# Hash-bucketed attention and two MLPs on one core: attention's result kept in feature rows, 32-column hash tiles, one rounding operation for k and q

## The chip, the cores and the metric

The kernel runs on one core of a Trainium2 chip. The metric is device time in microseconds (us). The kernel before takes 785.51 us (median of three runs, 785.46 to 785.63). The profiled execution took 787.35 us, and its span, from the first to the last instruction, is 785.6 us.

## The reference

Attention over 2 batches of 8 heads, 768 tokens, head size 64. A query sees only the keys of its own bucket; the bucket is given by the signs of six random projections. The result goes through two MLPs (1536 tokens, 512 to 2048 to 512), the first with softplus, the second with x * relu6(x + 3) / 6. The weights are float64.

```python
q_bits = (np.einsum('bhsd,dk->bhsk', q, proj) > 0)       # proj: 64 x 6
k_bits = (np.einsum('bhsd,dk->bhsk', k, proj) > 0)
mask = q_bucket[:, :, :, None] == k_bucket[:, :, None, :]
scores = np.where(mask, scale * q @ k.T, -1e9)
attn = exp(scores - max); attn = attn / (sum(attn) + 1e-9)
out = attn @ v                                            # then (B*S, H*D)
x = softplus(out @ w_in) @ w_out
y = (x @ w2_in * relu6(...) / 6) @ w2_out
```

## The kernel before

**Order of the work.** The program is not written in its final order. Every operation is added to a plan (`Schedule.add`) with a cost on each engine that may do it, its dependences and a priority. `Schedule.run` then plays the plan on modelled engines and emits the instructions, engine by engine, in the order that it finds. Priorities come from a head's number times `TH` plus an offset from `WHEN`. Each engine runs its own instructions in the emitted order, SyncE its DMA issues too.

**Precision.** TensorE multiplies in a rounded float32 format (F32R, one pass). So k and q are split into a rounded part and a remainder, and a score is the sum of two matmuls: `qa` with `ka` (L437), and `qb` with `kb` (L438). `qa` has the remainder of q in its upper 64 rows and the rounded, scaled q in the lower 64; `ka` has the rounded k twice. `qb` has the rounded q (a DMA copy, L366), `kb` the remainder of k (L361, shown as L254 kb); below them both have rows with hash bits, which subtract 2^33 for each bit that differs.

**`prepare(h)`** loads a head (two halves of `raw`, a doubled `rawk`, and v as `vx`), makes these operands, multiplies `raw` with the projections (`dot`, L379: two matmuls of 384 columns, each in a 64-column tile of TensorE), turns the products into bits in one VectorE operation (L401), and copies the bits into `qb` and `kb` with four DMAs (L410). Each operand has two buffers.

**`attend(h)`** goes through six query tiles of 128. For each: scores into two PSUM banks, the row maximum on VectorE (L451) and its conversion to bias and scale (L458), exp with its row sum on ScalarE (L466), six transposes by TensorE (L477), and a copy out of PSUM (`et`, L249 on ScalarE, L251 on VectorE; VectorE may take every third tile). Three pairs of banks serve scores and transposes, so the work goes in batches of three tiles. Then the product with v (`some`, L493, plain float32 in 64-column tiles, one half of the queries in each) goes into one of two further banks, named av and pre, which hash products use too. Its result has features in rows. It is copied to SBUF on ScalarE (`xa`), transposed by TensorE (`pt`, L515), multiplied by the reciprocals of the row sums (L519, L523) on VectorE into token rows (`xn`, L530), and for every pair of heads transposed back (`to_features`, `xt`, L557), rounded on ScalarE (`xh`) and subtracted on VectorE (`xl`).

**The MLPs** follow, group by group of 512 tokens: `hidden` (L662), `activation`, `project` (L755 and L757), `finish`. Part of the weights is converted from float64 by ScalarE and VectorE during attention, part at the start of the first MLP, when the SBUF of attention's tiles is free (`close_heads`, `close_attention`).

Of the kernel before, what the change touches and what calls it, by code (L numbers as in the profile page):

```python
# [9 lines left out]
F32 = mybir.dt.float32  # L10
# [23 lines left out]
EX = 3  # L34

TH = 16.41
WHEN = dict(load_p=-69.22, load_k=-58.24, load_q=23.18, load_v=-47.14, high_k=64.04, high_q=79.83, low_k=32.38, low_q=105.41, copy_q=116.1, dots=124.52, bits=46.23, send=11.13, scores=-1.98, max=-149.65, exp=-149.76, turn=-8.77, even=-56.85, values=53.65, back=58.37, rec=72.46, norm=75.82, x=27.98, x_high=21.57, x_low=7.85)
# [3 lines left out]
SAME = dict(A=0.13, D=0.05, P=0.1, T=0.0, S=0.0, H=0.0)  # L41

SWITCH = dict(rt=0.0, rc=0.138, tr=0.007, tc=0.145, cr=0.205, ct=0.156)
STAY = 10.971
ISSUE, SETUP, LANDED = 0.6, 1.3, 0.4
LANES = 8
TICK, WARM = 3.413, 0.374
START, EVERY = 33.82, 14.426
STEP = 8.253
PROJECT = 11.022  # L50
ACTIVATE = -66.584
FETCH = 125.921
AHEAD = -20.863


def f32(ap):
    return ap.bitcast(F32)
# [27 lines left out]
class Schedule:  # L85
# [24 lines left out]
    def run(self):  # L110
# [3 lines left out]
        while ready:  # L114
            options = []
            for op, times in ready.items():
                slot = self.slots(op)
                if slot is not None:
                    for e, t in times.items():
                        at, end, unit = max(free[e], slot, t), op.cost[e], e  # L120
                        if e == "T":
                            end += SWITCH.get(f"{mode}{op.mode}", 0.0)
                        if e == "T" and busy.get(int(at / TICK) - 1, 0.0) < WARM * TICK:
                            end *= 2
                        if op.dma:
                            at, end, unit = max(at, free["G"], lanes[-LANES]), ISSUE, "G"
                        options.append((op.prio, at, at + end, unit, e, op))
            if not options:
                raise RuntimeError("no operation can go on")
            end, unit = min((o[2], o[3]) for o in options)  # L130
            rivals = [o for o in options if o[3] == unit]
            soon = min(o[1] for o in rivals)
            rivals = [o for o in rivals if o[1] <= soon]

            late = lambda o: o[0] + (STAY if unit == "T" and o[5].mode != mode else 0.0)
            _, start, end, _, e, op = min(rivals, key=lambda o: (late(o), o[1]))
# [56 lines left out]
def lsh_attention_two_mlps(  # L193
# [25 lines left out]
    KB = D + ROWS  # L219
# [13 lines left out]
    open_pool("ps", ctx, space=PSUM)  # L233
    open_pool("tail", attention, side="right")
# [23 lines left out]
    plan.add(dict(P=1.0), lambda e: make_identity(nc, ident.ap), writes=[ident], prio=5)  # L258
# [6 lines left out]

    def set_rows(e):

        for u in range(P // ROWS):
            bounds = ((0.0, NB), (-TINY, NR), (0.0, P)) if u % 2 == 0 else ((-TINY, NB), (0.0, P))
            rows = thr.ap[u * ROWS : (u + 1) * ROWS, :]  # L270
            for i, (value, _) in enumerate(bounds):
                if i == 0:
                    nc.gpsimd.memset(rows, value)
                else:
                    nc.gpsimd.affine_select(
                        out=rows, in_=rows, compare_op=ALU.is_gt, fill=value, base=bounds[i - 1][1],
                        pattern=[[0, 1]], channel_multiplier=-1,
                    )
            nc.gpsimd.memset(top.ap[u * ROWS : (u + 1) * ROWS, :], -BIG if u % 2 else 1.0)

    plan.add(dict(P=0.9), set_rows, writes=[thr, top], prio=-3)
# [17 lines left out]

    qa, qb, ka, kb, vx = {}, {}, {}, {}, {}  # L300

    def prepare(h):
# [29 lines left out]
        wide, narrow = dict(A=0.864) if h else dict(A=0.864, D=0.587), dict(D=0.93)  # L332

        def scaled(e):
# [3 lines left out]
            else:  # L338
                nc.vector.tensor_scalar(o, i, SCALE, None, op0=ALU.mult)

        plan.add(wide, scaled, reads=[raw], writes=[qa[h]], prio=at + WHEN["high_q"])
        plan.add(
            narrow,
            lambda e: nc.vector.scalar_tensor_tensor(
                qa[h].ap[0:D, :], raw.ap[D:P, :], SCALE, f32(qa[h].ap[D:P, :]), op0=ALU.mult, op1=ALU.subtract
            ),
            reads=[raw, qa[h]], writes=[qa[h]], prio=at + WHEN["low_q"],
        )
        if h:
            plan.add(  # L350
# [3 lines left out]
        else:  # L354
            for s0, e in ((0, "D"), (D, "A")):
# [4 lines left out]
        plan.add(  # L360
            dict(D=0.85), lambda e: minus(e, kb[h].ap[0:D, :], raw.ap[0:D, :], f32(ka[h].ap[0:D, :])),  # L361
            reads=[raw, ka[h]], writes=[kb[h]], prio=at + WHEN["low_k"],
        )
        if h:
            plan.add(
                queue, lambda e: engines[e].dma_start(out=f32(qb[h].ap[0:D, :]), in_=f32(qa[h].ap[D:P, :])),  # L366
                reads=[qa[h]], writes=[qb[h]], prio=at + WHEN["copy_q"], dma=(0.8, 2.7),
            )
        else:
# [14 lines left out]
        plan.add(dict(T=0.646), dot, mode="c", reads=[raw, hashes], writes=[dots], prio=at + WHEN["dots"])  # L384
        if h == 0:
            for u in range(2):
                for n, x in enumerate((qb, kb)):
                    rows = slice((2 * u + n) * ROWS, (2 * u + n + 1) * ROWS)
                    plan.add(
# [5 lines left out]
                        reads=[dots, thr, top], writes=[x[h]], prio=at + WHEN["bits"],  # L395
                    )
            return
        bits = buffer("heads", [P, HALF], F32R, "bt", 2, f"bt{h}")
        plan.add(
            dict(D=0.585),  # L400
            lambda e: nc.vector.tensor_scalar(  # L401
                bits.ap, dots.ap[:, :HALF], thr.ap[:, 0:1], top.ap[:, 0:1], op0=ALU.is_gt, op1=ALU.mult
            ),
            reads=[dots, thr, top], writes=[bits], prio=at + WHEN["bits"],
        )
        for u in range(2):
            for n, x in enumerate((qb, kb)):
                plan.add(
                    queue,
                    lambda e, u=u, n=n, x=x: engines[e].dma_start(  # L410
                        out=f32(x[h].ap[D:KB, u * HALF : (u + 1) * HALF]),
                        in_=f32(bits.ap[(2 * u + n) * ROWS : (2 * u + n + 1) * ROWS, :]),
                    ),
                    reads=[bits], writes=[x[h]], prio=at + WHEN["send"], dma=(0.2, 1.95),
                )
# [4 lines left out]
    def attend(h):  # L420
        at = h * TH
        if h % 2 == 0:
            xn[h // 2] = buffer("tail", [P, NT, P], F32, "xn", 2, f"xn{h // 2}")
# [16 lines left out]
        for t in range(NT):  # L440
# [3 lines left out]
            for u in range(2):  # L444
                last_scores = plan.add(
                    dict(T=0.353), lambda e, sc=sc, t=t, u=u: scores(sc, t, u),
                    reads=[qa[h], qb[h], ka[h], kb[h]], writes=[sc], prio=step + WHEN["scores"],
# [6 lines left out]
                reads=[sc], writes=[nm], prio=step + WHEN["max"],  # L454
            )
            plan.add(
                dict(D=0.07),
# [4 lines left out]
                reads=[nm], writes=[bs], prio=step + WHEN["max"],  # L462
# [18 lines left out]
            def even(e, tp=tp, t=t):  # L481
# [4 lines left out]
                dict(A=0.692) if t % 3 else dict(A=0.692, D=0.867), even, reads=[tp], writes=[et[t // n]], prio=step + WHEN["even"],  # L486
# [12 lines left out]
        for c in range(0, NT, 2):  # L499
            last = [  # L500
                plan.add(
                    dict(T=1.29), mode="c", emit=lambda e, c=c: [some(c), some(c + 1)],
# [3 lines left out]
        xa = buffer("tail", [P, HALF], F32, "xa", 2, f"xa{h}")  # L506
        plan.add(
            dict(A=0.372), lambda e: cast(e, xa.ap, av.ap[:, :HALF]),
            reads=[av], writes=[xa], prio=at + WHEN["back"],
        )  # L510
        pt = buffer("ps", [P, 512], F32, ("pre", "av"), 1, f"pt{h}")

        def back(e):
            for i in range(n):
                nc.tensor.transpose(pt.ap[:, i * P : (i + 1) * P], xa.ap[:, i * P : (i + 1) * P], ident.ap)  # L515

        plan.add(dict(T=0.33), back, mode="t", reads=[xa, ident], writes=[pt], prio=at + WHEN["back"])
# [8 lines left out]
        x = xn[h // 2]  # L526

        def norm(e):
            place = x.ap.rearrange("p (u i) d -> p i u d", u=2)[:, :, :, (h % 2) * D : (h % 2 + 1) * D]
            nc.vector.tensor_tensor(  # L530
                place, pt.ap[:, :HALF].rearrange("p (i u d) -> p i u d", u=2, d=D),
                rec.ap.rearrange("p (u i) -> p i u", u=2).unsqueeze(3).to_broadcast([P, n, 2, D]), op=ALU.mult,
            )

        plan.add(dict(D=0.464), norm, reads=[pt, rec], writes=[x], prio=at + WHEN["norm"])
# [12 lines left out]
    def to_features(hp_all, first, n):  # L548
# [3 lines left out]
        pt = buffer("ps", [P, 512], F32, ("pre", "av"), 1, f"xt{hp_all}_{first}")  # L552
        place = lambda x: x[0, g].ap[:, hp, off * P : (off + n) * P]

        def turn(e):
            for i in range(n):
                nc.tensor.transpose(pt.ap[:, i * P : (i + 1) * P], xn[hp_all].ap[:, first + i, :], ident.ap)  # L557

        plan.add(dict(T=0.11 * n), turn, mode="t", reads=[xn[hp_all], ident], writes=[pt], prio=at + WHEN["x"])
        hi = plan.add(  # L560
            dict(A=0.052 + 0.106 * n), lambda e: cast(e, place(xh), pt.ap[:, : n * P]),
            reads=[pt], writes=[xh[0, g]], prio=at + WHEN["x_high"],
        )
        plan.add(
            dict(D=0.07 + 0.132 * n), lambda e: minus(e, place(xl), pt.ap[:, : n * P], f32(place(xh))),
            reads=[pt], writes=[xl[0, g]], prio=at + WHEN["x_low"], after=[hi],
# [175 lines left out]

# [138 lines left out]
```

## Time and profile before

| | us |
|---|---|
| median of three runs | 785.51 |
| profiled execution, its span | 787.35, 785.6 |
| TensorE matmul busy | 764.9 (97%) |
| VectorE busy | 529.0 (67%) |
| ScalarE busy | 485.0 (62%) |
| GpSimd busy | 9.5 (1%) |

The chain of work that ended last is 90% TensorE. Busy time of matmuls is from a start to a modelled end, and neighbours overlap; so what a group of matmuls costs is read from its start to the start of the next. Attention lasts from the start to about 245 us, in which TensorE has some waits in the first heads and few later. The DMA engines are busy for 0.41 of the stretch from 40 to 240 us.

### The profile page before, as it was taken

What the parts mean: (1) busy time and instruction counts of PE and PEld (TensorE: products, weight loads), DVE (VectorE), ACT (ScalarE), POOL (GpSimd) and SP (SyncE); (2) the same over time, 40 slices, a digit from 0 to 9 for tenths busy, and PEclk for the clock granted to TensorE, in tenths of its full rate; (3) what the DMA queues carried; (4) which work ended last, traced back from release to release, by engine and by line L of the source; (5) the groups of instructions that cost most, each with busy time, mean ns of one, the idle gap of its engine ahead of it and who ended that gap; (6) DMA issues with size and microseconds to landing.
All of it is one profiled execution on the core that took longest, in us unless ns stands there. A gap on an engine that the chain in (4) does not pass through costs nothing.

```text
span 785.6 us, 10356 instructions
## 1 busy us (share of the span) xinstructions
PE 764.9 (97%) x3808; PEld 599.1 (76%) x3808; DVE 529.0 (67%) x938; ACT 485.0 (62%) x821; POOL 9.5 (1%) x53
## 2 busy tenths in 40 slices
PE   4999999999999999999999999999999999999997
PEld 2677677677668788878888788878888888888886
DVE  6698887888986999964545899999932222232222
ACT  3789999998988778665556678766622322232222
POOL 1000000000000000000000000000000000000000
PEclk9999999999999999999999999999999999999999
DMA  5354454353323070000000555530000100010001
GB/s 165 108 162 116 115 165 120 110 163 118 80 73 134 28 294 1 1 0 1 1 0 1 188 196 191 177 107 1 1 0 14 42 0 1 1 53 1 1 0 54
DMA packets 26354, 58.61 MB, mean 75 GB/s; under 512 B 3584, under 2 KB 7552, under 8 KB 26304
## 3 DMA queue, kind: packets, MB, share of 16 engines
q1 hardware_dynamic: 22128, 49.56, 19.7%
q10 hardware_dynamic: 4176, 8.39, 3.4%
q8 instruction: 30, 0.49, 0.3%
q14 instruction: 20, 0.16, 0.1%
HBM read 48.89 MB, written 3.15 MB: 66 GB/s over the span
## 4 chain that ended last, share of the span: by engine, by line
PE 90%; ACT 4%; DVE 3%; issue 2%; DMA 1%; SPq 0%; ACTq 0%; DVEq 0%
PE ph L662 34%; PE acc L755 17%; PE acc L757 17%; PE tp L477 7%; PE av L493 6%; PE sc L437 4%; PE sc L438 3%; ACT e L466 2%; DVE nm L451 2%; PE xt L557 1%; ACT ka L249 1%; PE pt L515 1%; PE d L379 1%; DMA raw<-in_q_dram 1%; ACT et L249 0%
## 5 line engine op out<-in xcount | busy, mean ns | idle before, releaser
L662 PE MATMUL ph<-xh,w 128*128 128x512 f32 x768 | 239.1, 393 | 0.0
L662 PEld LDWEIGHTS ph<-xh,w 128*128 128x128 f32 x768 | 143.8, 188 | 31.7
L662 PE MATMUL ph<-xl,w 128*128 128x512 f32 x384 | 150.2, 391 | 0.0
L691 DVE SCALAR_TENSOR_TENSOR ml<-me,ph 128x512 f32<-128x512 f32 x48 | 33.1, 690 | 116.0 <-ACT me L686 115.8
L686 ACT ACTIVATE me<-ph,three 128x512 f32<-128x512 f32 x48 | 33.0, 687 | 124.2 <-PE ph L662 120.7
L466 ACT ACTIVATE e<-sc,bs 128x768 f32<-128x768 f32 x96 | 94.0, 986 | 19.0 <-DVE bs L458 19.0
L451 DVE TENSOR_REDUCE nm<-sc 128x1 f32<-128x768 f32 x96 | 88.7, 951 | 20.8 <-PE sc L438 20.6
L755 PE MATMUL acc<-gh,w 128*128 128x512 f32 x384 | 98.8, 395 | 0.1
L757 PE MATMUL acc<-w,gh 128*128 128x512 f32 x384 | 97.4, 392 | 0.0
L477 PEld LDWEIGHTS tp<-ident,e 128*128 128x128 f32 x576 | 63.3, 142 | 29.3 <-ACT e L466 20.2
L755 PEld LDWEIGHTS acc<-gh,w 128*128 128x128 f32 x384 | 70.9, 188 | 19.1 <-ACT gh L249 2.8
L757 PEld LDWEIGHTS acc<-w,gh 128*128 128x128 f32 x384 | 72.1, 188 | 16.2
L662 PEld LDWEIGHTS ph<-xl,w 128*128 128x128 f32 x384 | 72.1, 188 | 16.0
L477 PE MATMUL tp<-ident,e 128*128 128x128 f32 x576 | 76.6, 281 | 4.9 <-ACT e L466 3.8
L437 PE MATMUL sc<-ka,qa 128*128 128x384 f32 x192 | 69.1, 360 | 0.1
L493 PE MATMUL av<-et,vx 128*64 128x384 f32 x384 | 68.8, 494 | 0.0
L438 PE MATMUL sc<-kb,qb 96*128 96x384 f32 x192 | 65.3, 340 | 0.8 <-DVE kb L391 0.7
L249 ACT ACTIVATE et<-tp 128x768 f32<-128x768 f32 x82 | 62.2, 815 | 2.4 <-PE tp L477 2.3
L722 DVE SCALAR_TENSOR_TENSOR me<-mu,me 128x512 f32<-128x512 f32 x48 | 33.3, 693 | 33.1 <-ACT mu L717 33.0
L249 ACT ACTIVATE gh<-ml 128x512 fp32r<-128x512 f32 x48 | 30.2, 629 | 38.8 <-DVE ml L734 38.6
L755 PE MATMUL acc<-gl,w 128*128 128x512 f32 x192 | 53.4, 392 | 0.7 <-ACT xh L249 0.7
L757 PE MATMUL acc<-w,gl 128*128 128x512 f32 x192 | 53.1, 391 | 0.0
(65 smaller groups left out, 957.8 us busy)
## 6 DMA issues: line engine op xcount, KB each, us to landing
raw<-in_moe_w_out_dram SPq DMA_DIRECT2D x30, 512.0 KB, 3.5
raw<-in_moe_w_in_dram SPq DMA_DIRECT2D x18, 512.0 KB, 4.3
raw<-in_moe_w_in_dram ACTq DMA_DIRECT2D x14, 512.0 KB, 4.8
rawk<-in_kv_dram SPq DMA_DIRECT2D x15, 384.0 KB, 5.0
raw<-in_kv_dram SPq DMA_DIRECT2D x16, 192.0 KB, 3.2
raw<-in_q_dram SPq DMA_DIRECT2D x16, 192.0 KB, 3.7
vx<-in_kv_dram SPq DMA_DIRECT2D x16, 192.0 KB, 3.0
out_dram<-y SPq DMA_DIRECT2D x12, 256.0 KB, 2.1
```

Of the source, the lines that this page charges most:

```text
L249: nc.scalar.activation(out, in_, AF.Copy)
L437: nc.tensor.matmul(o, qa[h].ap[:, qs], ka[h].ap[:, cs], start=True, stop=False)
L438: nc.tensor.matmul(o, qb[h].ap[0:KB, qs], kb[h].ap[0:KB, cs], start=False, stop=True)
L451: lambda e, sc=sc, t=t: nc.vector.reduce_max(nm.ap[:, t, 0:1], sc.ap[:, :, :HALF], axis=AX.XY, negate=True),
L466: lambda e, sc=sc, ex=ex, t=t: nc.scalar.activation(ex.ap.rearrange("p (u k) -> p u k", u=2), sc.ap[:, :, :HALF], AF.Exp, bias=bs.ap[:, t, ...
L477: nc.tensor.transpose(o, ex.ap[:, c * P : (c + 1) * P], ident.ap)
L493: nc.tensor.matmul(av.ap[u * D : (u + 1) * D, :HALF], vx[h].ap[:, c, :], et[u].ap[:, c, :], start=(c == 0), stop=(c == NT - 1),)
L662: nc.tensor.matmul(bank(), w[:, a, :], x[b].ap[:, kc, :], start=(kc + i == 0), stop=(kc == KC - 1 and i == 2))
L691: lambda e: nc.vector.scalar_tensor_tensor(l.ap, e1.ap, 6.0, bank(), op0=ALU.min, op1=ALU.mult),
L722: lambda e: nc.vector.scalar_tensor_tensor(e1.ap, u.ap, -1.0, e1.ap, op0=ALU.add, op1=ALU.subtract),
L755: nc.tensor.matmul(o, w.ap[:, a, cs], b.ap, start=st, stop=sp)
L757: nc.tensor.matmul(o, b.ap[:, cs], w.ap[:, a, :], start=st, stop=sp)
```

## The change

1. `attend`: the reciprocals of the row sums go by DMA to DRAM (`row`) and come back repeated over 64 rows (`wide`). The result of the product with v is multiplied by them straight from PSUM, with features in rows, and two DMAs put it into the pair's tile `xn`, now [128 features, 768 tokens]. The copy `xa`, the transposes `pt` and `xt`, and `xn` in token rows are gone; `to_features` rounds and subtracts from SBUF.
2. The product with v is added in groups of three (`GROUP`) instead of two key tiles.
3. From the second head on, the hash product is four matmuls of 192 columns, each in a 32-column tile (`dot4`). The comparison is on 192 columns. Its result goes by one DMA to DRAM (`sent`) and by two into `qb` and `kb`. Hash rows are 16 instead of 32, so the second score matmul has 80 rows instead of 96.
4. From the second head on, k and q are rounded by one ScalarE operation of 128 rows with a scale for each row (`both`), and their remainders are made by one VectorE operation into `kb`. A DMA then moves q's remainder to the upper half of `qa`.
5. The first head's scores depend on the parts of the bits that they read. The copy of the exp transposes and the first head's scaling of q may go to VectorE in every tile.
6. MLP: at the end of a group, two column blocks are copied by one operation (first MLP); the first product of a group is added in two parts; in the last group the third column block is done and stored first.
7. The plan's priorities, its costs for VectorE, and its choice among waiting operations (`LEAN`, `LOOK`) have other values.

```diff
-TH = 16.41
+GROUP = 3
+WIDE = 1
+TH = 21.889
...
-START, EVERY = 33.82, 14.426
+START, EVERY = 26.69, 13.768
...
         if h:
+            plan.add(
+                dict(A=0.864), lambda e: nc.scalar.activation(qa[h].ap, raw.ap, AF.Copy, scale=both.ap[:, 0:1]),
+                reads=[raw, both], writes=[qa[h]], prio=at + WHEN["high_q"],
+            )
...
+            rest = plan.add(
+                dict(D=0.93),
+                lambda e: nc.vector.scalar_tensor_tensor(
+                    kb[h].ap, raw.ap, both.ap[:, 0:1], f32(qa[h].ap), op0=ALU.mult, op1=ALU.subtract
+                ),
+                reads=[raw, both, qa[h]], writes=[kb[h]], prio=at + WHEN["low_q"],
+            )
+            moved = [
+                plan.add(
+                    queue, lambda e: engines[e].dma_start(out=f32(qa[h].ap[0:D, :]), in_=f32(kb[h].ap[D:P, :])),
+                    writes=[qa[h]], uses=[kb[h]], prio=at + WHEN["low_k"], dma=(0.8, 2.7), after=[rest],
+                )
+            ]
...
+        def dot4(e):
+            for u in range(4):
+                nc.tensor.matmul(
+                    dots.ap[u * ROWS : (u + 1) * ROWS, :QT], hash4.ap, raw.ap[:, u * QT : (u + 1) * QT],
+                    start=True, stop=True,
+                )
...
+            lambda e: engines[e].dma_start(out=sent.ap.rearrange("u n r c -> (u n r) c"), in_=f32(bits.ap)),
...
+                    out=f32(x[h].ap[D:KB, :]).rearrange("r (u c) -> r u c", u=4),
+                    in_=sent.ap[:, n].rearrange("u r c -> r u c"),
...
-            dict(A=0.372), lambda e: cast(e, xa.ap, av.ap[:, :HALF]),
...
-                nc.tensor.transpose(pt.ap[:, i * P : (i + 1) * P], xa.ap[:, i * P : (i + 1) * P], ident.ap)
...
+                out=row.ap.rearrange("u p i -> p u i"), in_=rec.ap.rearrange("p (u i) -> p u i", u=2)
...
+                    out=wide.ap[u * D : (u + 1) * D], in_=row.ap[u].partition_broadcast(D)
...
+            lambda e: nc.vector.tensor_tensor(
+                xa.ap, av.ap[:, :HALF].rearrange("p (i q) -> p i q", q=P), wide.ap.rearrange("p q i -> p i q"),
+                op=ALU.mult,
+            ),
...
+                    out=x.ap[rows, u * HALF : (u + 1) * HALF], in_=xa.ap[u * D : (u + 1) * D].rearrange("p i q -> p (i q)")
...
-                nc.tensor.transpose(pt.ap[:, i * P : (i + 1) * P], xn[hp_all].ap[:, first + i, :], ident.ap)
```

## Rows read from the trace of the kernel before

**Rows 1.** Busy time by stretch: length, PE, PEld, DVE, ACT, POOL, PEclk, DMA share, GB/s.
```profile
40.00:240.00 200.00, 196.15 (x1288) 143.26 (x1288) 170.78 (x323) 181.44 (x317) 6.34 (x26) 1.00 0.41 120
280.00:320.00 40.00, 40.00 (x175) 32.22 (x174) 39.89 (x75) 30.67 (x56) 0.00 (x0) 1.00 0.24 94
520.00:770.00 250.00, 249.31 (x1088) 203.88 (x1087) 103.41 (x173) 80.12 (x127) 0.00 (x0) 1.00 0.03 11
```

**Rows 2.** Waits of TensorE over the span: total us, times, longest us.
```profile
PE tp L477 <- ACT e L466: 3.8, 4, 2.2
PE d L379 <- PE av L493: 2.3, 4, 0.6
PE sc L438 <- DVE kb L391: 0.7, 1, 0.7
```

**Rows 3.** TensorE by time in one head: start us, busy us, instructions.
```profile
100.06 0.42 PE L437 MATMUL sc<-ka,qa 128*128 128x384 f32 x1
...
102.24 0.49 PE L515 MATMUL pt<-ident,xa 128*128 128x128 f32 x3
102.66 2.80 PE L493 MATMUL av<-et,vx 128*64 128x384 f32 x16
105.39 2.18 PE L477 MATMUL tp<-ident,e 128*128 128x128 f32 x18
107.33 0.42 PE L437 MATMUL sc<-ka,qa 128*128 128x384 f32 x1
...
109.37 0.33 PE L438 MATMUL sc<-kb,qb 96*128 96x384 f32 x1
109.63 1.51 PE L493 MATMUL av<-et,vx 128*64 128x384 f32 x8
110.97 0.81 PE L379 MATMUL d<-raw,hash 128*64 128x384 f32 x4
111.72 2.55 PE L477 MATMUL tp<-ident,e 128*128 128x128 f32 x18
114.02 0.42 PE L437 MATMUL sc<-ka,qa 128*128 128x384 f32 x1
```

**Rows 4.** The same in the next head, to the start of the head after it.
```profile
120.76 0.60 PE L557 MATMUL xt<-ident,xn 128*128 128x128 f32 x4
121.19 0.82 PE L477 MATMUL tp<-ident,e 128*128 128x128 f32 x6
...
123.33 0.44 PE L557 MATMUL xt<-ident,xn 128*128 128x128 f32 x2
123.52 0.42 PE L437 MATMUL sc<-ka,qa 128*128 128x384 f32 x1
...
124.41 1.51 PE L493 MATMUL av<-et,vx 128*64 128x384 f32 x8
126.50 0.87 PE L379 MATMUL d<-raw,hash 128*64 128x384 f32 x4 [0.58 <-PE av L493]
...
129.23 0.42 PE L437 MATMUL sc<-ka,qa 128*128 128x384 f32 x1
```

**Rows 5.** By time: a row sum on GpSimd, and a DMA issue on SyncE.
```profile
99.10 0.40 POOL L519 TENSOR_SCALAR rec<-den 128x6 f32<-128x6 f32 x1 [1.42 <-ACT e L466]
...
116.01 0.50 SPq L366 DMA_DIRECT2D qb<-qa  x1
```

**Rows 6.** Groups of instructions, 20 to 276 us: busy us, mean ns | idle before.
```profile
L249 ACT ACTIVATE et<-tp 128x768 f32<-128x768 f32 x82 | 62.2, 815 | 2.4 <-PE tp L477 2.3
L254 DVE TENSOR_TENSOR kb<-raw,ka 64x768 fp32r<-64x768 f32 x14 | 13.2, 941 | 0.0
L249 ACT ACTIVATE xa<-av 128x384 f32<-128x384 f32 x16 | 7.8, 489 | 0.0
```

**Rows 7.** DMA issues: count, KB each, median us from issue to landing.
```profile
rawk<-in_kv_dram SPq DMA_DIRECT2D x15, 384.0 KB, 5.0
qb<-qa SPq DMA_DIRECT2D x15, 192.0 KB, 2.9
kb<-bt SPq DMA_DIRECT2D x30, 48.0 KB, 2.0
```

More of the change, by code (lines that the diff above doesn't have):

```diff
@@ L233, in lsh_attention_two_mlps @@
     open_pool("ps", ctx, space=PSUM)
+    open_pool("rows", ctx, space=bass.MemoryType.DRAM)
     open_pool("tail", attention, side="right")
@@ L266, in set_rows, with steps @@
+    def steps(rows, bounds):
+        for i, (value, _) in enumerate(bounds):
+            if i == 0:
+                nc.gpsimd.memset(rows, value)
+            else:
+                nc.gpsimd.affine_select(
+                    out=rows, in_=rows, compare_op=ALU.is_gt, fill=value, base=bounds[i - 1][1],
+                    pattern=[[0, 1]], channel_multiplier=-1,
+                )
     def set_rows(e):
         for u in range(P // ROWS):
-            bounds = ((0.0, NB), (-TINY, NR), (0.0, P)) if u % 2 == 0 else ((-TINY, NB), (0.0, P))
@@ L270, in set_rows @@
[L270 to L279, printed above, removed]
@@ L281, in lsh_attention_two_mlps, with set_line @@
-    plan.add(dict(P=0.9), set_rows, writes=[thr, top], prio=-3)
+            rows = slice(u * ROWS, (u + 1) * ROWS)
+            steps(thr.ap[rows, :], ((0.0, NB), (-TINY, NR), (0.0, P)) if u % 2 == 0 else ((-TINY, NB), (0.0, P)))
+            nc.gpsimd.memset(top.ap[rows, :], -BIG if u % 2 else 1.0)
+    def set_line(e):
+        low, high = (line.ap[:, i, :].rearrange("o (u r) -> o u r", r=ROWS) for i in range(2))
+        nc.gpsimd.memset(line.ap[:, 0, :], 0.0)
+        for first in (NB, BR):
+            nc.gpsimd.memset(low[:, :, first : first + NB], -TINY)
+        nc.gpsimd.memset(high[:, :, :BR], 1.0)
+        nc.gpsimd.memset(high[:, :, BR:], -BIG)
@@ L282, in lsh_attention_two_mlps, with set_both @@
+    both = buffer("heads", [P, 1], F32, "both", 1, "both")
+    def set_both(e):
+        nc.gpsimd.memset(both.ap[0:D, :], 1.0)
+        nc.gpsimd.memset(both.ap[D:P, :], SCALE)
+    plan.add(dict(P=0.2), set_both, writes=[both], prio=-2)
     p32 = buffer("heads", [P, NB], F32, "p32", 1, "p32")
@@ L297, in lsh_attention_two_mlps, with set_hash4 @@
     plan.add(dict(D=0.6), set_hashes, reads=[p32], writes=[hashes], prio=-39)
+    hash4 = buffer("heads", [P, ROWS], F32, "hash4", 1, "hash4")
+    def set_hash4(e):
+        nc.gpsimd.memset(hash4.ap, 0.0)
+        for n in range(2):
+            nc.gpsimd.tensor_copy(hash4.ap[:, n * BR : n * BR + NR], hashes.ap[:, n * ROWS : n * ROWS + NR])
+    plan.add(dict(P=0.9), set_hash4, reads=[hashes], writes=[hash4], prio=4)
     qa, qb, ka, kb, vx = {}, {}, {}, {}, {}
+    parts = {}
     def prepare(h):
@@ L446, in attend @@
                     dict(T=0.353), lambda e, sc=sc, t=t, u=u: scores(sc, t, u),
-                    reads=[qa[h], qb[h], ka[h], kb[h]], writes=[sc], prio=step + WHEN["scores"],
+                    reads=[qa[h], ka[h]], writes=[sc], uses=[qb[h], kb[h]], prio=step + WHEN["scores"],
+                    after=[
+                        op for i, x in enumerate((qb[h], kb[h])) for op in x.writers
+                        if op not in parts.values() or op is parts[i, (t // n, u)[i]]
+                    ],
                 )
@@ L453, in attend @@
                 ),
[L454 removed]
+                reads=[sc], writes=[nm], prio=step + WHEN["max"], after=nm.writers[:1],
             )
             plan.add(
[L457 removed]
+                dict(D=0.069),
                 lambda e, t=t: nc.vector.scalar_tensor_tensor(
@@ L461, in attend @@
                 ),
-                reads=[nm], writes=[bs], prio=step + WHEN["max"],
+                writes=[bs], prio=step + WHEN["max"], after=[nm.writers[-1]], uses=[nm],
             )
@@ L498, in attend @@
         last = ()
-        for c in range(0, NT, 2):
+        for c in range(0, NT, GROUP):
             last = [
                 plan.add(
-                    dict(T=1.29), mode="c", emit=lambda e, c=c: [some(c), some(c + 1)],
+                    dict(T=0.645 * GROUP), mode="c", emit=lambda e, c=c: [some(c + i) for i in range(GROUP)],
                     reads=[*et, vx[h]], writes=[av], prio=at + c * TH / NT + WHEN["values"], after=last,
@@ L525, in attend @@
         )
[L526 to L532, printed above, removed]
-            )
-        plan.add(dict(D=0.464), norm, reads=[pt, rec], writes=[x], prio=at + WHEN["norm"])
+        row = buffer("rows", [2, P, n], F32, "row", 2, f"row{h}")
+        wide = buffer("tail", [P, P, n], F32, "wide", WIDE, f"wide{h}")
+        xa = buffer("tail", [P, n, P], F32, "xa", 1, f"xa{h}")
+        plan.add(
+            dict(S=0.6),
+            lambda e: engines[e].dma_start(
+                out=row.ap.rearrange("u p i -> p u i"), in_=rec.ap.rearrange("p (u i) -> p u i", u=2)
+            ),
+            reads=[rec], writes=[row], prio=at + WHEN["rec"], dma=(0.6, 3.5),
+        )
+        for u in range(2):
+            plan.add(
+                dict(S=0.6),
+                lambda e, u=u: engines[e].dma_start(
+                    out=wide.ap[u * D : (u + 1) * D], in_=row.ap[u].partition_broadcast(D)
+                ),
+                reads=[row], writes=[wide], prio=at + WHEN["rec"], dma=(0.65, 3.2),
+            )
+        plan.add(
+            dict(D=0.585),
+            lambda e: nc.vector.tensor_tensor(
+                xa.ap, av.ap[:, :HALF].rearrange("p (i q) -> p i q", q=P), wide.ap.rearrange("p q i -> p i q"),
+                op=ALU.mult,
+            ),
+            reads=[av, wide], writes=[xa], prio=at + WHEN["norm"],
+        )
+        x, rows = xn[h // 2], slice(h % 2 * D, (h % 2 + 1) * D)
+        for u in range(2):
+            plan.add(
+                dict(S=0.6),
+                lambda e, u=u: engines[e].dma_start(
+                    out=x.ap[rows, u * HALF : (u + 1) * HALF], in_=xa.ap[u * D : (u + 1) * D].rearrange("p i q -> p (i q)")
+                ),
+                reads=[xa], writes=[x], prio=at + WHEN["back"], dma=(0.45, 2.2),
+            )
         return last_scores
@@ L741, in activation, with store @@
         return gh, gl
+    def store(g, c, e, after, prio):
+        b, cc = divmod(4 * g + c, NT)
+        y = buffer("m", [P, 512], F32, "ye"[c // 2], 2, f"y{g}_{c}")
+        tile_of = acc[1, g][c // 2]
+        copied = plan.add(
+            {e: dict(A=0.478, D=0.602)[e]}, lambda e: cast(e, y.ap, tile_of.ap[:, c % 2, :]),
+            uses=[tile_of], writes=[y], prio=prio, after=after,
+        )
+        dst = out[b * S : (b + 1) * S, :].rearrange("(p c) e -> p c e", c=NT)[:, cc, :]
+        plan.add(
+            dict(S=0.6), lambda e: nc.sync.dma_start(out=dst, in_=y.ap), reads=[y], prio=prio, dma=(1.0, 2.1)
+        )
+        return copied
     def project(layer, g, f, gh, gl, prio):
@@ L764, in project @@
                     dict(T=0.229 * len(cs)), lambda e, i=i, cs=cs: [some(i, c) for c in cs],
-                    reads=[w, gl if i == 2 else gh], writes=acc[layer, g], prio=prio, after=last,
+                    reads=[w, gl if i == 2 else gh], writes=[acc[layer, g][c // 2] for c in cs[::2]] if len(cs) > 1 else acc[layer, g],
+                    prio=prio, after=last,
                 )
```

184 lines of the change are left out of this document (98 added, 86 removed).

## The prediction

> **What bounds the kernel now.** I read the busy time by stage first. The reader is to see three stages there: attention, in which TensorE is busy 196.15 of 200 us with ScalarE at 181.44 and VectorE at 170.78 close behind; the start of the first MLP, where TensorE has 40.00 of 40 and VectorE 39.89 of 40; and the rest, where TensorE is full and the two others have room [rows 1]. TensorE's time is thus the time of the kernel, and a saving on another engine shows only where TensorE waits for that engine. The waits of TensorE come second: 3.8 us for exp, 2.3 us in four pieces in which a hash product stands behind a product with v, 0.7 us in the first head [rows 2]. All that is little, so the question of the change is which TensorE instructions go. For that I read the TensorE instructions of two heads in order of time, from the start of one group to the start of the next, because the busy spans overlap by a drain [rows 3, 4].
>
> One head reads as: scores of three query tiles, a filling, 18 transposes of the exp tiles; the same again. From 100.06 to 114.02 a head takes 13.96 us, and the next one, in which the pair's result is transposed, 15.21 us, to 129.23 [rows 3, 4]; the mean is 14.59.
>
> **The change part by part.** All sums are made against the profiled execution, 787.35 us (span 785.6 and 1.75 around it). The median of the runs shown is 785.51, so 1.84 less; I take the same saving off both.
>
> *Transposes of a head's result (pt).* Three go per head: 102.24 to 102.66, 0.42 us [rows 3]. Fourteen of the sixteen heads show 0.42 to 0.47, the last two 0.25 among MLP work: 6.4 us. What is left is a direct step from scores to the product with v. Such a step stands at 109.37: 0.26 to the next start, where a score matmul takes 0.18 (eleven from 107.33 to 109.37, and a step of their own), so 0.08 comes back, 14 times, 1.1 us. Net 5.3.
>
> *Transposes of the pair (xt).* Four take 0.43 (120.76 to 121.19), two take 0.19 (123.33 to 123.52) [rows 4]; over the eight pairs the start-to-start times add up to 4.9 us. All of it goes, as no TensorE work takes its place: 4.9.
>
> *Hash in 32-column tiles.* Today two matmuls of 384 columns lie side by side in 64-column tiles: 110.97 to 111.72, 0.75, with 0.8 every second time, mean 0.77 [rows 3]. Eight pairs' halves of the v product of the same shape take 2.73 for 16 instructions [rows 3], so 0.68 a pair, and 0.09 is overhead. Four matmuls of 192 columns fully side by side would cost 0.34 + 0.09 = 0.43; no better than two at a time 0.77; one after another 4 x 0.34 + 0.09 = 1.45. No row shows a 32-column tile. I take 0.43, because the 64-column pair, the nearest row, does run fully side by side. Fifteen heads (the first keeps its form): 15 x 0.34 = 5.1; ends 0 and -10.2.
>
> A new step comes in with it: hash and v product have one shape today and two after. The steps between shapes that rows show cost 0.08 (scores to v product, above). I take 0.08, 15 x 0.08 = 1.2 us against the change; ends 0 and 0.58, the latter being the length of a whole wait of TensorE for its own v product, at 126.50 [rows 4]. The Trainium skill (TensorEngine Tiling (Array Packing), section Key Properties) says that a change of the tiling mode, not of the tile alone, drains TensorE. A drain does not contradict the 0.08 in this trace; taken at the 0.58 instead it would make this term 8.7 us, and that is a rival below.
>
> *The four waits of a hash product behind the v product.* The row at 126.50 has 0.58, and the group ahead of it runs 2.09 from 124.41 where the same eight instructions elsewhere take 1.34: 0.75 each, 3.0 for the four [rows 2 to 4]. They stand only in heads in which xt has just used one of the two PSUM banks that hash, v product, pt and xt share. After the change only hash and v product share them. But the v result is now held until its multiplication. I take half, 1.5; ends 0 and 3.0.
>
> *Products with v in threes.* The blocks of 16 and 8 instructions [rows 3] become 12 and 12: two blocks either way, no saving. Ends plus and minus one step, 16 x 0.08 = 1.3.
>
> *VectorE and ScalarE.* Per head ScalarE loses the copy of the v result (489 ns), VectorE one of its two remainder operations (941 ns) and some 0.26 of the hash comparison [rows 6]; the multiplication stays one VectorE operation, now from PSUM. At 14.59 per head ScalarE is at 13.2 and VectorE at 12.5 [rows 1]; after, 12.7 and 11.3 in a head of about 13.5: 94% and 84%. The copy of the exp transposes (815 ns [rows 6]) may now go to either in every tile, so one moved evens them out. Alone this is worth nothing, as TensorE is ahead of both; but the cover gets thinner. From the end of the scores (109.55) to the end of the transposes (114.02) pass 4.47, and those transposes take 2.30 where an unhindered batch takes 1.94 (105.39 to 107.33): they were already waiting for exp [rows 3]. After, one half has a filling of 2.05 + 0.43 + 0.16, with transposes 4.58; the other 2.05 + 0.08 and 1.94 = 4.07, which the exp chain stretches to 4.47. A head is then 2 x 2.2 + 4.58 + 4.47 = 13.45, against 14.59: 1.14 a head, 17 in fifteen heads. That is the terms above with all of the 3.0 and no price for thinner cover. ScalarE at 94% will not hit every exp on time: I take 2.0 us off; ends 0 and 8 (0.27 for each of 30 batches).
>
> *New DMAs.* Per head: remainder of q, hash bits out to DRAM and back in two, the reciprocals out and back in two, the result in two; four bit copies go. Nine SyncE issues become thirteen. Whom do they hold up? The reciprocals: the sum starts at 99.10 [rows 5], the v product that needs them ends at 111.72 at the latest, 11 to 12 us later [rows 3]. Two transfers in a row, each 2.0 to 5.0 by the nearest landings [rows 7], and three issues of 0.50 [rows 5] need 5.5 to 11.5: covered in the middle, 0. If late, the multiplication and one bank wait, not TensorE's next scores. The operands: buffers of the next head come free when the scores of the head before last end (109.55), and are needed at 129.23, 19.7 later, about 18 after the change. Rounding 0.8, remainder 0.94, a 192 KB move 2.9, a landing of the bits of 2.0 and two issues of 0.50 are about 8 [rows 5 to 7]. Covered twice over: 0; the cover is gone at +10 us.
>
> *Start, group ends, tail.* In the first head the scores may start on parts of the bits (0.7 [rows 2]); against that stand more GpSimd work and two SyncE issues. I take +0.5; ends -2 and +2. Merged copies at the ends of the MLP groups: TensorE shows 0.69 idle in 250 there [rows 1]; 0, ends -2 and +1. The last column block still ends on ScalarE and a store: 0.
>
> Sum: 5.3 + 4.9 + 5.1 - 1.2 + 1.5 + 0.5 - 2.0 = 14.1 us. Profiled execution 773.3; median 771.4, said as 771.
>
> **The rivals.**
> (a) *Narrow tiles don't pay.* Either four 32-column tiles run no better than two at a time (the 5.1 is lost), or the new step costs 0.58 (7.5 more than taken). For: no row has such a tile. Against: 0.08 at every step that is shown. 776 to 779; both 784.
> (b) *The exp chain becomes the bound, and the kernel is slower.* The place is ScalarE between the scores and the first exp of a batch. If one operand rounding or copy of about 0.82 [rows 6] stands ahead of the exps in each of 30 batches, TensorE waits 25 us and the time is 771 + 25 = 796. It decides from 14.1 / 30 = 0.47 us per batch. For: 2.30 instead of 1.94 already, and ScalarE at 94%. Against: TensorE waits only 3.8 for exp in all [rows 2], and VectorE has room.
> (c) *Given back in the first MLP.* VectorE is full from 280 to 320 [rows 1]; if it enters with more left over, TensorE waits there. For: attention gets shorter while the weight conversions don't get fewer, some 15 us of VectorE time less in which to do them. Against: 0.94 + 0.26 a head, 18 us in all, go from VectorE before that. If half its saving is missing, 7 to 8 us: 779.
> (d) *More than counted.* All four waits go, thinner cover costs nothing, start gains 2: 771 - 1.5 - 2 - 1.5 = 766; with a better order in the first heads, if the longest wait for exp, 2.2 [rows 2], goes too, 764.
>
> **How the numbers follow.** Forecast 771, own range 766 to 776: 0.50. (a) and (c), 776 to 784: 0.23. (d) under 766: 0.12. No change, 784 to 787: 0.04. Slower, (b) in some strength: 0.11. The 8 in 10 reach from 764 to 784; what is outside is the good end of (d), no change, and (b). About 0.2%, 1.6 us, is what a measurement can tell from no change. Faster by over that 0.85, within it 0.04, slower 0.11.
>
> **What would show it.** No pt and xt rows; hash 0.4 to 0.5 from start to start (0.77 or more: (a)); 12 and 12 v instructions; a head of 13.3 to 13.8; the end of the last scores 14 us earlier; TensorE idle in attention under 3%; MLP stages as long as now (longer with VectorE full: (c)). I am wrong in kind if transposes of exp take 2.6 or more per 18 in most batches (b), or if scores wait for kb or qa behind a DMA, which would break the cover of 10 us.

## The result, and the profile after

The changed kernel takes 793.85 us (median of four runs, 791.98 to 795.79); the kernel before takes 785.53 beside it. The ratio is 1.0106, 95% interval 1.0082 to 1.013. It is slower by 8.3 us where 771 and a gain were forecast. The profiled execution took 794.03, its span 792.0. Of all runs one, the second of e5_after_th23 (809.05 us, against 795.64 in the first), is left out as slow.

First the stages, in the columns of [rows 1]: three stretches that answer to those rows, then attention cut at the start of its 15th batch of scores and at the end of its last scores.

```profile
40.00:240.00 200.00, 184.98 (x1213) 129.09 (x1213) 182.58 (x335) 144.82 (x255) 4.60 (x26) 0.98 0.63 159
...
280.00:320.00 40.00, 40.00 (x175) 32.04 (x174) 39.74 (x75) 31.91 (x56) 0.00 (x0) 1.00 0.27 107
...
520.00:770.00 250.00, 250.00 (x1091) 204.39 (x1090) 108.99 (x183) 83.69 (x131) 0.00 (x0) 1.00 0.04 15
...
40.00:111.39 71.39, 70.26 (x470) 48.50 (x468) 69.78 (x130) 54.29 (x97) 1.96 (x11) 1.00 0.71 181
111.39:247.68 136.29, 121.14 (x784) 85.08 (x783) 119.43 (x219) 94.47 (x167) 2.64 (x15) 0.97 0.56 141
247.68:792.00 544.32, 539.76 (x2359) 435.17 (x2358) 330.51 (x562) 279.26 (x455) 0.33 (x2) 1.00 0.16 54
```

The MLPs are as before: 544.3 us from the last scores to the end, against 785.6 - 240.7 = 544.9. All of the loss lies in attention, whose scores end at 247.68 instead of 240.7. In attention ScalarE fell from 181 to 145 of 200 us, VectorE rose from 171 to 183, and TensorE stood for 15 us instead of 4. Up to 111.39 VectorE is busy for 69.78 of 71.39 us, 98%. The 15th batch still starts 2.6 us earlier than before (111.39 against 114.02), the last one 7.4 later (245.38 against 237.96).

The waits of TensorE, as in [rows 2], with two rows of ScalarE at xh:

```profile
PE tp L559 <- ACT e L548: 14.3, 8, 5.6
ACT xh L256 <- DMA xn<-xa: 12.7, 8, 3.5
...
ACT xh L256 <- issue: 6.8, 1, 6.8
...
PE sc L514 <- DVE kb L461: 1.1, 1, 1.1
```

The four waits for the v product are gone; 14.3 us for exp have come, where 3.8 were. ScalarE stands 19.5 us before xh, the rounding of the attention result.

TensorE in one head, as in [rows 3]:

```profile
104.37 0.42 PE L513 MATMUL sc<-ka,qa 128*128 128x384 f32 x1
...
106.40 0.34 PE L514 MATMUL sc<-kb,qb 80*128 80x384 f32 x1
106.67 0.53 PE L449 MATMUL d<-raw,hash 128*32 128x192 f32 x8
107.13 2.16 PE L575 MATMUL av<-et,vx 128*64 128x384 f32 x12
109.22 2.38 PE L559 MATMUL tp<-ident,e 128*128 128x128 f32 x18
111.39 0.44 PE L513 MATMUL sc<-ka,qa 128*128 128x384 f32 x1
```

pt and xt are gone, the hash takes 0.46 from start to start, the v product comes in twelves of 2.09. What TensorE was to lose, it lost.

VectorE and ScalarE from 20 to 260 us, as in [rows 6], and the transfers, as in [rows 7]:

```profile
L258 DVE COPY et<-tp 128x768 f32<-128x768 f32 x58 | 54.4, 949 | 5.1 <-PE tp L559 4.8
...
L256 ACT ACTIVATE et<-tp 128x768 f32<-128x768 f32 x37 | 30.0, 810 | 10.3 <-PE tp L559 9.9
...
L400 DVE SCALAR_TENSOR_TENSOR kb<-raw,both,qa 128x768 fp32r<-128x768 f32 x14 | 14.2, 1011 | 0.0
...
L616 DVE TENSOR_TENSOR xa<-av,wide 128x384 f32<-128x384 f32 x15 | 10.3, 685 | 0.0
```

```profile
wide<-row SPq DMA_DIRECT2D x32, 96.0 KB, 2.9
xn<-xa SPq DMA_DIRECT2D x32, 96.0 KB, 5.0
...
sent<-bt SPq DMA_DIRECT2D x15, 96.0 KB, 5.3
...
row<-rec SPq DMA_DIRECT2D x16, 3.0 KB, 4.9
```

Of 96 copies of exp transposes 59 went to VectorE (58 in this stretch). In the kernel before it was 14:

```profile
L251 DVE COPY et<-tp x14: 937/942/958, 18.2 to 243.4; 128x768 f32<-128x768 f32 x14
```

The transfer into `xn` lands after 2.2 to 8.4 us (median 5.0); the plan reckons 2.2.

What the longest wait looks like, in order of time (start, busy, instruction, idle before it):

```profile
139.33 0.70 DVE L616 TENSOR_TENSOR xa<-av,wide 128x384 f32<-128x384 f32 x1
...
139.55 0.98 ACT L548 ACTIVATE e<-sc,bs 128x768 f32<-128x768 f32 x1
...
140.34 1.23 SPq L626 DMA_DIRECT2D xn<-xa  x2
...
143.69 2.16 PE L575 MATMUL av<-et,vx 128*64 128x384 f32 x12
144.19 0.15 DVE L540 SCALAR_TENSOR_TENSOR bs<-nm 128x2 f32<-128x2 f32 x1
...
149.43 0.94 ACT L256 ACTIVATE xh<-xn 128x512 fp32r<-128x512 f32 x2 [6.83 <-issue]
...
150.28 0.97 ACT L548 ACTIVATE e<-sc,bs 128x768 f32<-128x768 f32 x1
...
151.40 3.85 PE L559 MATMUL tp<-ident,e 128*128 128x128 f32 x18 [5.55 <-ACT e L548]
```

The multiplication ends at 140.03 and its two transfers are issued from 140.34 on. ScalarE has three operations left before xh, which needs those transfers, and then stands 6.83 us. The row puts this wait down to `issue`, that is, to nothing that the profile shows; but the second transfer was issued at 141.0 and landed 8.4 us later, at 149.4, just as xh starts. Behind xh in its queue is the first exp of the next batch, whose scale and bias VectorE had ready at 144.34. It starts at 150.28, and TensorE has stood 5.55 us by then. The chain of waits has the first of the two transfers here:

```profile
140.34 7.61 DMA xn<-xa
147.94 1.49 issue
149.43 0.07 ACT xh L256
```

In all, xn<-xa makes 11.4% of the chain from 40 to 250 us, VectorE's row maxima and copies of exp transposes 25.8%, and TensorE's transposes, v products and scores 20.6%; in the kernel before, the last three are 69.9% of the chain from 40 to 240.

### The profile page after: what moved, and what is told of

The parts are those of the page before. It is cut to its first block, busy times and chain, and to the rows that moved or that the text cites. A ratio compares the mean times of both kernels' runs of the same rounds, so it can differ in the third digit from the quotient of the medians.

```text
span 792.0 us, 10430 instructions
## 1 busy us (share of the span) xinstructions
PE 761.5 (96%) x3772; PEld 589.9 (74%) x3772; DVE 550.8 (70%) x963; ACT 450.8 (57%) x753; POOL 9.5 (1%) x63
## 4 chain that ended last, share of the span: by engine, by line
PE 75%; DVE 12%; DMA 5%; issue 3%; ACT 3%; SPq 1%; ACTq 0%; DVEq 0%
PE ph L752 33%; PE acc L859 17%; PE acc L861 17%; DVE nm L531 4%; DVE et L258 3%; PE tp L559 3%; DMA xn<-xa 3%; ACT e L548 2%; PE av L575 2%; DMA row<-rec 1%; PE sc L513 1%; PE sc L514 1%; DVE xa L616 1%; DVE bs L540 1%; DVE w L261 1%
## 5 line engine op out<-in xcount | busy, mean ns | idle before, releaser
L548 ACT ACTIVATE e<-sc,bs 128x768 f32<-128x768 f32 x96 | 94.0, 984 | 27.5 <-DVE bs L540 27.2
L559 PEld LDWEIGHTS tp<-ident,e 128*128 128x128 f32 x576 | 64.8, 146 | 47.1 <-ACT e L548 42.5
L559 PE MATMUL tp<-ident,e 128*128 128x128 f32 x576 | 82.8, 289 | 17.6 <-ACT e L548 14.3
L513 PE MATMUL sc<-ka,qa 128*128 128x384 f32 x192 | 71.2, 371 | 0.5 <-DVE et L258 0.3
L514 PE MATMUL sc<-kb,qb 80*128 80x384 f32 x192 | 66.7, 347 | 1.1 <-DVE kb L461 1.1
L258 DVE COPY et<-tp 128x768 f32<-128x768 f32 x59 | 55.4, 949 | 5.9 <-PE tp L559 5.7
```

The source lines that it names most:

```text
L258: engines[e].tensor_copy(out, in_)
L513: nc.tensor.matmul(o, qa[h].ap[:, qs], ka[h].ap[:, cs], start=True, stop=False)
L514: nc.tensor.matmul(o, qb[h].ap[0:KB, qs], kb[h].ap[0:KB, cs], start=False, stop=True)
L548: lambda e, sc=sc, ex=ex, t=t: nc.scalar.activation(ex.ap.rearrange("p (u k) -> p u k", u=2), sc.ap[:, :, :HALF], AF.Exp, bias=bs.ap[:, t, ...
L559: nc.tensor.transpose(o, ex.ap[:, c * P : (c + 1) * P], ident.ap)
```

## The experiments

Each time stands beside runs of the kernel before on the same chip (785.7 to 785.9); ratios are to it, with the 95% interval. The runs e1, e2, e9, e13 and e14 leave out a dependence: they price a wait and are not kernels to use.

**e1_xh_own_data**, to take away the wait at xh alone:

```diff
+        same = lambda: ident.ap.unsqueeze(1).to_broadcast([P, n, P])
-            ... lambda e: cast(e, place(xh), x.ap[:, cols]),
+            ... lambda e: cast(e, tiles(place(xh)), same()),
-            lambda e: minus(e, place(xl), x.ap[:, cols], f32(place(xh))),
+            lambda e: minus(e, tiles(place(xl)), same(), f32(tiles(place(xh)))),
```

> Same instructions in the same order on every engine as the changed kernel, but the rounding xh and its remainder xl read a constant tile instead of the pair's result, so they wait for no DMA (the output is that of another input). Theory Q (ScalarE stands in its queue at xh until the transfer xn<-xa has landed, with exps behind it): the long waits of TensorE for exp in the trace of the changed kernel (5.6, 3.4, 1.7, 1.4 and one more, 12.2 us from 40 to 240 us) go, and with them the stretched start of the batch after each; 793.9 goes to 778 to 783. Theory V (VectorE is full, because it has 59 copies of exp transposes instead of 13): it stays full, 790 or more. Theory R (the multiplication waits for the repeated reciprocals and holds VectorE): 790 or more, as that wait stays.

780.47 us, ratio 0.9937 (0.9922 to 0.9951): 13.4 below the changed kernel. The same two stretches of attention, by its own batches:

```profile
40.00:111.12 71.12, 70.02 (x468) 48.47 (x467) 69.93 (x131) 54.09 (x97) 2.25 (x11) 1.00 0.70 182
111.12:234.00 122.88, 119.42 (x784) 83.39 (x782) 118.31 (x219) 94.27 (x167) 2.66 (x15) 1.00 0.63 156
```

The first is what it was, the second 13.4 us shorter. Theory Q stands. VectorE is as full as it was, so V is not needed for these 13.4.

**e2_no_chain**, also without the wait for the reciprocals:

```diff
-                xa.ap, ..., wide.ap.rearrange("p q i -> p i q"),
+                xa.ap, ..., ident.ap.unsqueeze(1).to_broadcast([P, n, P]),
```

> As the run before, and the multiplication of the product with v reads the same constant tile instead of the repeated reciprocals, so that nothing on an engine waits for the transfers row, wide and xn (all are still made). Same order of instructions. Theory Q: within 2 us of the run before. Theory R: clearly below it, by 5 us or more. Theory V: both 790 or more.

778.37, ratio 0.9903 (0.9889 to 0.9918): 2.1 less. R is a small part.

**e3_plan_xn_8us**:

```diff
-                reads=[xa], writes=[x], prio=at + WHEN["back"], dma=(0.45, 2.2),
+                reads=[xa], writes=[x], prio=at + WHEN["back"], dma=(0.45, 8.0),
```

> The changed kernel with one number in its plan: the transfer xn<-xa is reckoned with 8.0 us instead of 2.2 (the trace shows 2.2 to 8.4, median 5.0), so that the plan sets xh later. Nothing is left out. Theory Q: TensorE's waits for exp behind xh go; 778 to 784, with noise from a reordered plan of 3 us either way. Theory V: 790 or more.

794.71, ratio 1.0117 (1.01 to 1.0134): a miss for Q as I put it. No wait at xh is left in the trace, but TensorE waits 8.5 us for exp elsewhere; VectorE is at 181 of 200 with 46 copies. Exps now wait 38.9 us for the row maxima, where they waited 27.2. The chain around the longest gap between batches (102.44 to 113.37) has a row transfer of 6.86 us and a wide one of 2.38, then ScalarE's rounding of k and q; but that rounding reads neither, and ScalarE stood only 0.22 us before it. So the wait at xh went with the new order and the time did not; which of its choices cost that is not shown.

**e4_et_scalar**:

```diff
-                dict(A=0.692, D=0.867), even, ...
+                dict(A=0.692) if t % 3 else dict(A=0.692, D=0.867), even, ...
```

> The changed kernel, with the copy of the exp transposes allowed on VectorE in every third tile only, as before. Theory V: VectorE goes from 0.91 to about 0.80 busy between 40 and 240 us, the undisturbed batches from 7.0 to 6.8 us or less; 782 to 787. Theory Q: the waits behind xh stay, and ScalarE, which has them, gets more to do: 790 to 798.

775.99 (773.45 to 777.44), ratio 0.9871 (0.985 to 0.9891). With nothing left out this is faster than both kernels, and below what either theory allowed.

```profile
40.00:240.00 200.00, 196.03 (x1303) 139.16 (x1304) 173.64 (x334) 179.94 (x309) 4.97 (x28) 1.00 0.70 170
```

22 copies are on VectorE, it is 0.87 busy, ScalarE 0.90, TensorE 0.98. ScalarE waits 1.6 us for xn at xh instead of 19.5, although row, wide and xn are still there:

```profile
ACT xh L256 <- DMA xn<-xa: 1.6, 4, 0.9
```

Here such a place looks so:

```profile
107.66 0.68 DVE L616 TENSOR_TENSOR xa<-av,wide 128x384 f32<-128x384 f32 x1
...
108.52 1.19 SPq L626 DMA_DIRECT2D xn<-xa  x2
...
112.01 0.63 ACT L256 ACTIVATE xh<-xn 128x512 fp32r<-128x512 f32 x1 [0.27 <-issue]
```

**e5_after_th23** and **e6_scalar_th23**, another order for the changed kernel and for e4_et_scalar:

```diff
-TH = 21.889
+TH = 23.5
```

> The changed kernel with the plan's spacing of heads TH at 23.5 instead of 21.889: the same operations, in another order on every engine, 70 copies of exp transposes on VectorE instead of 59. It tells how far a time hangs on the one plan. Theory V+ (too many copies on VectorE make it full, the multiplication and its transfer late, and so ScalarE's wait at xh): 790 or more, as there are more copies. Theory P (the order of this one plan is unlucky): anywhere from 773 to 800, 775 to 785 likeliest.

> The same other spacing with the copies restricted as in the run e4_et_scalar (16 on VectorE). Theory V+: 772 to 780, as there. Theory P: no relation, 775 to 795.

795.64 (a single run, so no interval) and 783.37, ratio 0.9974 (0.9947 to 1.0001). The first is within V+; the second is a miss, 3 us above its 772 to 780. Both lie within the ranges of P too. The difference between the two, 12.3 us, has the sign of the one between the changed kernel and e4_et_scalar (17.9) and two thirds of its size; the order alone moves the changed kernel by 1.8 us and e4_et_scalar by 7.4.

**e7_et_none**:

```diff
-                dict(A=0.692, D=0.867), even, ...
+                dict(A=0.692), even, ...
```

> The changed kernel, with all copies of exp transposes on ScalarE (0 on VectorE). Theory V+: 772 to 782; ScalarE, at 0.90 busy with 22 copies on VectorE, comes to 0.98 and starts to hold back the exps, so rather the upper half. Theory Q alone (the wait at xh does not hang on VectorE): 788 or more.

795.83, ratio 1.013 (1.0075 to 1.0185). By its time this is where theory Q alone had it, but ScalarE waits only 4.2 us at xh in its trace; so V+ misses and Q doesn't explain it (e14_none_no_chain, below).

**e8_before_et_free**, one line of the change in the kernel before:

```diff
-                dict(A=0.692) if t % 3 else dict(A=0.692, D=0.867), even, ...
+                dict(A=0.692, D=0.867), even, ...
```

> The kernel before, with this one part of the change: the copy of the exp transposes may go to VectorE in every tile (57 do instead of 14). It has no transfer between the product with v and the rounding xh. Theory Q+V+ (a full VectorE hurts only through the chain multiplication, transfer, xh): within 3 us of before. Rival: a full VectorE delays the row maxima and so the exps by itself: 790 to 800.

802.85, ratio 1.0219 (1.0189 to 1.0249). The rival was right: 57 copies on VectorE cost the kernel before 17 us, with no transfer behind them. This too is one order against another; what the trace adds is that the engine is full and who waits for it. Its attention and ScalarE's exps:

```profile
40.00:240.00 200.00, 192.39 (x1203) 131.83 (x1202) 194.36 (x345) 145.13 (x261) 5.43 (x24) 1.00 0.42 118
```

```profile
ACT e L466 <- DVE bs L458: 51.1, 31, 4.4
```

VectorE is 0.97 busy, and exps wait 51.1 us for the row maxima. In the kernel before it was 19.0:

```profile
ACT e L466 <- DVE bs L458: 19.0, 14, 4.5
```

**e9_scalar_xh_own**, the edits of e1_xh_own_data and e4_et_scalar together:

> The order of e4_et_scalar (22 copies on VectorE), and xh and xl read a constant tile as in e1_xh_own_data (the output is that of another input). If the wait at xh is a consequence of the full VectorE, little is left to gain: 773 to 776, as ScalarE waits 1.6 us at xh in e4_et_scalar. If it is a cost of its own, about 13 us as at 59 copies: 762 to 766.

774.01, ratio 0.9841 (0.9825 to 0.9856). That fills the table:

| | ScalarE waits at xh | it doesn't | difference |
|---|---|---|---|
| 59 copies on VectorE | 793.85 | 780.47 | 13.4 |
| 22 copies | 775.99 | 774.01 | 2.0 |
| difference | 17.9 | 6.5 | |

Most of the wait at xh (11.4 of 13.4 us) is there only with the plan in which VectorE is full.

**e10_scalar_landings**, e4_et_scalar with `dma=` of 8.0, 5.0, 4.0, 5.0 and 5.0 for xn, row, wide, sent and the move of q's remainder:

> e4_et_scalar with five transfers reckoned in the plan by the traces: xn<-xa 8.0 us instead of 2.2, row 5.0 instead of 3.5, wide 4.0 instead of 3.2, sent 5.0 instead of 2.1, the move of q's remainder 5.0 instead of 2.7. If wrong landing times matter beside the copies: 768 to 774. If they don't once VectorE has room: 773 to 784, that is, e4_et_scalar and the scatter of a new order.

776.83, ratio 0.9879 (0.9862 to 0.9895): as e4_et_scalar. In this order, in which the engines have room, the plan's landing times make no difference.

**e11_scalar_64rows**, e4_et_scalar with the operand code of the kernel before:

```diff
-                dict(A=0.864), lambda e: nc.scalar.activation(qa[h].ap, raw.ap, AF.Copy, scale=both.ap[:, 0:1]),
+            plan.add(dict(A=0.864), scaled, reads=[raw], writes=[qa[h]], ...)
+            plan.add(narrow, ... qa[h].ap[0:D, :], raw.ap[D:P, :], SCALE, f32(qa[h].ap[D:P, :]) ...)
+            plan.add(dict(D=0.85), lambda e: minus(e, kb[h].ap[0:D, :], raw.ap[0:D, :], f32(ka[h].ap[0:D, :])), ...)
```

> e4_et_scalar without part 4 of the change: q's rounding and the two remainders in 64-row operations as before, no move of q's remainder by DMA. VectorE gets 15 x 0.94 = 14 us back to do. If VectorE is what the part relieves, and what counts: 780 to 790. If the part is worth nothing by itself: 772 to 780.

783.85, ratio 0.9971 (0.9959 to 0.9983): 7.9 above e4_et_scalar, VectorE at 185 of 200, ScalarE waiting 5.6 us at xh again. Part 4 is worth something, through VectorE, as far as one order can tell.

**e12_scalar_other_third**:

```diff
+                dict(A=0.692) if t % 3 != 1 else dict(A=0.692, D=0.867), even, ...
```

> e4_et_scalar with the second tile of each three free for VectorE instead of the first (16 copies there). If few copies are what counts: 773 to 784 (e4_et_scalar and e6_scalar_th23 are the scatter). If e4_et_scalar was one lucky order: 785 or more.

797.14, ratio 1.0138 (1.0092 to 1.0184): a miss. Few copies alone don't give the gain.

**e13_third_no_chain** and **e14_none_no_chain**, e12_scalar_other_third and e7_et_none with the edits of e2_no_chain:

> The order of e12_scalar_other_third (16 copies on VectorE), with xh, xl and the multiplication reading a constant tile as in e2_no_chain (the output is that of another input). If the landings hold the engines there: 775 to 782. If the order is slow by itself: 790 or more.

> The order of e7_et_none (0 copies on VectorE), with the same waits taken away. There ScalarE waited 4.2 us at xh and was 0.91 busy. If landings hold it: 778 to 785. If a full ScalarE delays the exps: 790 or more.

796.16, ratio 1.0128 (1.0034 to 1.0222), and 791.18, ratio 1.0057 (1.0032 to 1.0082). These two orders are slow without those landings, which cost e7_et_none 4.6 us; the 1.0 of e12_scalar_other_third is less than its two runs differ by (794.34, 799.93). Attention in e7_et_none and its waits of TensorE from 40 to 250 us:

```profile
40.00:240.00 200.00, 189.01 (x1239) 131.62 (x1239) 150.93 (x298) 182.50 (x314) 6.19 (x27) 0.99 0.67 160
```

```profile
PE tp L559 <- ACT e L548: 8.8, 9, 1.5
```

By its time e14_none_no_chain lies where a full ScalarE was put, but ScalarE is hardly fuller in e7_et_none than in e4_et_scalar (182.5 against 179.9). In both slow orders TensorE takes some batches tile by tile instead of three at a time. Which of the plan's choices does that was not tried.

## Why the prediction was wrong

**Right: what TensorE loses.** pt and xt are gone. The hash costs 0.46 and the step into it 0.09 (106.40 to 106.67 less 0.18), 0.55 together; 0.51 were taken. So rival (a) is out. The v products come in 2.09 each (2.05). The Trainium skill (TensorEngine Tiling (Array Packing), section Key Properties) has a change of tiling mode drain TensorE; nothing here contradicts it, but what it costs at these steps is 0.09, not the 0.58 of the rival. The four waits behind the v product are gone with 3.0, twice what I took. The first scores start at 9.11 instead of 10.2: 1.1 for the 0.5. The MLPs neither gained nor lost: rival (c) is out. With VectorE relieved and xh made to wait for nothing (e9_scalar_xh_own) the time is 774.01, 11.9 under the kernel before beside it, against 14.1 summed. Counted from the other end: of the 22.9 us between 771 and 793.85, 13.4 go with the wait at xh, 6.5 more with e4_et_scalar's order, and 3.0 stay.

**The step that failed: "one moved evens them out. Alone this is worth nothing, as TensorE is ahead of both".** I moved one copy of six per head from ScalarE to VectorE. The plan, left free, moved about three, and VectorE became the engine that bounds attention: 98% busy up to 111 us, a head in 14.06 (84.35 us for six heads from 27.04), where 13.45 were summed. In the kernel before that edit alone, with the order that comes of it, costs 17 us (e8_before_et_free); it never belonged among the terms of nothing. In the changed kernel it costs 17.9 in this order and 12.3 in another (e5_after_th23 against e6_scalar_th23). These are prices of whole orders, not of a copy: e12_scalar_other_third and e7_et_none, with 16 and 0 copies there, are as slow.

**And with it: "If late, the multiplication and one bank wait, not TensorE's next scores".** I asked who needs the reciprocals and the result, and found cover. I did not ask what stands behind the waiting instruction on its own engine. Behind xh on ScalarE stand the exps; that is worth 13.4 us. The Trainium skill (TensorE: Matmul & The Clock Gate, section Architectural detail: the array is 16× 32×32, not 1× 128×128) says that ScalarE's and VectorE's queues are strictly first in, first out. The trace agrees: at 149.43 ScalarE had stood 6.83 us, 5.09 of them with an exp ready behind xh. The list of new transfers also adds up wrong: nine issues per head, less four, plus the nine that it names are fourteen, not thirteen. That is not what cost the time: SyncE stands 42.5 us before the two wide issues until row has landed, with later issues behind them, and 47.1 in e4_et_scalar, which is the fastest with nothing left out.

**Rival (b)** named the place (ScalarE between scores and exp) and a time of 796, but priced it as one operation of 0.82 in each of 30 batches. It was a wait for a landing in some of them, 5.55 us at the longest; that its 796 lies near is luck. Its sign, 2.6 us or more for 18 transposes in most batches, did not come: about half of them take 2.57 or more. The cover "gone at +10 us" for the operands was not what decided: scores wait 1.1 us for an operand, in the first head. In another order it does give way a little (e5_after_th23: 3.3 us for kb<-sent).

**Thinner cover** was set at 2 us, its end at 8. With VectorE relieved the head is 13.85 on the mean (26.77 to 227.58 for 14.5 heads) instead of 13.45: 6 us over fifteen heads, inside the bounds and three times what I took.

**A term that is missing.** Part 7 of the change, other priorities and so another order, has no term in the sum. Orders of the same operations differ here by up to 21 us (below), more than the gain that was forecast, and no run has the new priorities alone.

**Open:** why the orders of e7_et_none and e12_scalar_other_third are slow with few copies. The scatter of orders, 7 us between e4_et_scalar and e6_scalar_th23 and up to 21 with e12_scalar_other_third, is as large as the change itself. TensorE's mean granted clock from 40 to 240 us is 0.99 and 0.98 in those two, 1.00 in e4_et_scalar, so a part of their loss can be the slower clock; how much was not measured. A single order tells little about a part, e11_scalar_64rows included.

## What to carry to other kernels

Where an engine with 98% of its time in use is relieved, the next two can become the bound: add up their busy time per stage for every operation that may now choose its engine, at both choices, before any of it is costed at nothing. Where a path through an engine is replaced by a transfer, find the instruction that waits for the landing and read what is queued behind it on its engine, not only who needs the data. And when the order comes from a planner, run the change in a second order before believing either sign.

## What the runs showed of the hardware

The 3 KB transfer of the reciprocals (128 x 6 values, put in another order on the way) takes 4.9 us in the median, as long as 96 KB into xn (5.0) and longer than 96 KB out of DRAM (2.9).

After the idle stretch TensorE ran slow for a while. In the changed kernel it stood from 145.9 to 151.40, and then had:

```profile
146.00:151.40 5.40, 0.01 (x1) 0.01 (x1) 1.30 (x4) 1.97 (x5) 0.00 (x0) 0.69 0.56 131
151.40:155.00 3.60, 3.60 (x18) 3.60 (x19) 2.55 (x5) 2.63 (x5) 0.00 (x0) 0.52 0.21 68
155.00:160.00 5.00, 5.00 (x36) 3.13 (x35) 4.26 (x9) 4.16 (x8) 0.06 (x1) 1.00 0.14 31
```

While TensorE stood, the granted clock fell to the lower of its two levels (1.2 of 2.4 GHz): it is 0.52 in the mean of the next stretch, in which 18 transposes took 3.60 us from start to start, where other batches that had to wait for exps take up to 2.7 and unhindered ones 1.94. So this wait was paid for again behind it. Its length alone doesn't tell: after 3.35 us (to 183.58, changed kernel) the clock was 1.00 and 18 transposes took 2.57, after 2.02 us (to 98.99, e3_plan_xn_8us) it was 0.62 and they took 3.45.
